# Leaving out the masked 64x64 blocks of a causal score matrix, with 64x64 transposes, in a fused retention and GELU kernel

## The chip, the cores and the metric

The kernel runs on one core of a Trainium2 chip. The time is device microseconds from one execution; three runs of the kernel before gave 203.04, 203.36 and 203.53 us, median 203.36. The profile is of a further execution. PE is TensorE (with PEld, its weight loads), DVE is VectorE, ACT is ScalarE, POOL is GpSimd and SP is SyncE, which issues most DMAs.

## The reference

Eight heads (H) of 64 channels (D), four sequences (B) of 768 tokens, in float32. First a recurrence with a decay for each head, then a feed-forward block on its output:

```python
for t in range(S):
    state = gamma[None, :, None, None] * state + einsum('bhd,bhe->bhde', k[:, :, t], v[:, :, t])
    y[:, :, t] = scale * einsum('bhd,bhde->bhe', q[:, :, t], state)
x = y.transpose(0, 2, 1, 3).reshape(B * S, H * D)
h = x @ w_in                                             # 512 x 2048
g = 0.5 * h * (1.0 + tanh(c * (h + 0.044715 * h**3)))
out = g @ w_out                                          # 2048 x 512
```

The recurrence is computed by chunks of tokens: inside a chunk, y is (q k^T, with decay and a causal mask) times v; what lies ahead of the chunk comes in through a state of 64x64 for each head.

## The kernel before

The tokens are cut into six chunks c of 128; a chunk of all four sequences (b = 0 to 3) is 512 rows of x. For each chunk there is an attention part and a MoE part, and the MoE matmuls of one chunk fill PE while the attention of the next waits for other engines.

**Attention of chunk c** (`att`, line 779). `load_in` (765) loads q, k and v of one b, 128 tokens x 8 heads x 64 floats, in one DMA each; in chunks 3 to 5 (`BLK`) `q_load` (704) loads q of all b in 16 DMAs (L713), in an order that lets DVE transpose it in 32x32 blocks (`trq`, L689). `cast` (226) makes f16 of it, with decay factors from the table `cst` by L234 or without by L217/L219. `mm_T` (266, L269) transposes q and k, two heads at a time, as 128x128 on PE; in chunks 3 to 5 only k. `evT`/`evTk` copy the transposes from PSUM into `qkT`. `mm_A` (273, L278) makes the scores: 16 matmuls for a b, each 64 channels x 64 keys x 128 queries, on one of the four 64x64 quarters of the array; the two heads of a pair (j) go to two PSUM banks. `ev_A1` (328, L329) multiplies them on DVE with `mask`, which holds the triangle and the decay, and writes `a` in f16. `mm_yc` (289, L297) starts y with state times q; `mm_yi` (306, L309) adds a times v, 8 matmuls of 128 keys x 64 channels x 128 queries for a b, two at a time on the two column halves. `ev_Y1` (331, L336) scales y with `dec` and writes `x`. `mm_s` (318, L320) makes k^T v for the new state, and `ev_S2` (338, L341) adds it.

**MoE of chunk c.** Chunk 0 and the first product of chunk 1 are plain matmuls (L407 and L553). The others are a seven-product scheme for 2x2 blocks (`PROD`, line 511): `m1w_mm` (525, L530) with its sums `xs` and `u_w`, GELU on ACT (L423), `m2w_mm` (539, L542) with sums `s_g` and `t_w` (L432, on DVE and POOL). Partial results go from PSUM by ACT copies (`snap`, L217, into `st` or `o`) and DVE adds (`add`, L432).

**What sets the order.** Every operation is an `Item` with needs, buffers and the engines that may do it (`KIND`, 600). The order and the engine of each are written out in the string `ORDER` (16): a letter for the engine, a number for the item. The code at line 1230 walks through it; a buffer or bank is taken from the slot that came free first. So each engine runs its instructions in a fixed order and waits at each for its inputs. SP issues its loads in one chain (`prev`). PSUM has eight bank slots; `SIZE` (129) holds the numbers of the other buffers, five of `qkT` among them.

Of the kernel before, what the change touches and what calls it, by code (L numbers as in the profile page):

```python
# [16 lines left out]
v8 g0 v9 p168 a167 a7 w3 p173 g10 g1 g2 p171 g3 g4 a172 p178 p184 w1 p188 a187 p176 v169  # L17
v170 p180 a179 p182 p190 a189 v174 p192 a191 v175 v181 p206 p208 v143 v147 v148 v151 v152
v159 v160 v139 a183 g5 p210 v135 v162 v154 p194 p186 p196 a177 a193 a185 a209 v144 p198 p212
a211 v163 p222 p224 a205 p200 p214 a197 a223 a199 p226 p202 g6 a213 s11 v23 v140 v141 s12  # L20
s13 p228 p230 s14 p232 a207 a201 v149 a229 a225 p216 a221 a227 s15 s16 g28 g25 a195 v24 s17
s18 s19 p204 a203 s20 s21 v164 a215 v26 v155 p803 p234 a233 p236 s22 g31 g34 p804 p805 s35
s36 p806 p807 v136 a235 s37 a231 p218 p808 p809 p220 p810 p811 a219 v27 s38 s39 s40 p238
v237 p812 a813 a217 p815 v146 a816 v156 p243 v242 p818 p241 v240 v239 p246 v245 p257 v244
p821 p822 p823 v29 v30 p260 v259 p262 a261 a819 v138 s41 s42 v32 v33 s43 v157 s44 s45 g57
g58 s46 s47 s814 p824 a825 v166 v150 v158 p248 p272 p274 a271 a273 p276 p253 a275 v247 v252
p278 a277 p280 a279 p256 v255 s820 p251 p258 v249 v250 p282 p284 a281 p268 v254 p264 a283
a263 a48 p266 a51 a52 v265 p270 v165 v269 a54 g55 v267 p286 p288 g49 p290 p325 a287 a289
g305 v303 v324 p335 p292 s60 s61 s62 g50 p320 s826 v304 v334 a285 v53 v56 a291 p330 a319
a329 p294 p296 p298 s63 a293 v307 v308 a295 p333 s64 s65 a297 g311 g312 g59 v332 p338 v336  # L30
p323 v337 p300 a299 p302 a301 v322 g313 v321 p827 p328 v331 p340 p339 v326 p342 g314 p348
p350 p352 v327 v341 v347 v351 p346 p344 g315 p828 a69 g71 v343 v137 v316 v345 g353 g355 s66
p830 p831 a829 a81 a73 s817 s67 a75 a77 g79 v142 p376 s68 p357 p374 a375 s85 p393 g354 p833
g318 v832 p834 g310 p391 s86 v349 p398 a392 g72 p381 g356 g80 s87 v145 v317 v394 a358 v377
a382 p379 a380 p396 p362 a363 a835 v78 p359 v360 v70 a361 a397 p836 p366 v153 g76 p386 p837
a83 a395 v309 p364 a365 p839 a378 v161 p400 p383 v387 g306 v367 v384 a399 a838 p369 p840
a368 a388 a385 v401 p403 p372 s88 s89 v370 a373 v404 p408 a409 p389 p406 g84 a405 p410 p415
a371 g425 g426 g427 a402 p452 a390 v82 a407 a416 v411 v74 g433 p842 p843 s90 p413 a414 a412
g434 p447 p442 a441 p457 v429 v841 a98 v844 s845 v446 p420 v451 v456 v421 g430 p417 p846
a422 a100 v418 p455 v453 p460 p445 v458 v443 v459 s91 p847 a848 v444 g97 p850 s92 v454 s849  # L40
p423 a424 a419 g428 g437 p851 a852 p450 p461 v448 p462 p472 p468 p464 p470 v449 v471 a94
g438 a106 p474 v463 v469 p466 v465 s93 p853 p854 p856 p857 g102 v467 g104 v435 p481 p530
p496 a497 s110 g475 p479 a480 p498 s111 a858 a96 g476 v439 g477 g436 v855 a108 v473 g101
g478 a531 v95 v499 s112 s113 s114 g119 g109 v482 p859 p503 p532 g432 g121 a504 a500 s115
s116 p501 a502 v533 p860 a534 p564 p484 v563 v99 v431 p508 v509 p486 p569 v568 v107 p535
a487 a485 p505 v506 a536 a861 p862 p488 a507 v489 p537 p863 v440 p491 v492 a483 a490 p539
a538 p579 a510 p494 p511 a512 g553 a495 p865 g105 a578 p513 p866 v540 v864 a514 v551 p515
v103 v120 p574 p520 a493 g547 a573 v516 a517 p518 a521 a519 g552 g122 g549 p542 p869 p686
a685 v867 v543 s117 s868 p525 v526 a527 p522 v523 s118 a544 a524 p870 a871 s872 p572 v571
a541 p582 g548 p528 a529 v580 p545 a546 g561 v581 v570 v555 v557 g556 v559 g560 g550 g562  # L50
g558 p873 p874 a875 p577 v575 a123 p567 v565 v576 v566 p876 p877 p584 p583 p594 p588 p592
p586 v124 v585 a131 a133 a127 a129 v587 p590 v589 g554 p596 v593 v591 p879 a125 p880 a881
v595 p882 p635 a636 v878 p601 a602 p603 p883 p618 a619 p691 v604 g597 p620 p625 g599 v132
v690 g598 p885 v621 g600 g134 p640 a605 p637 v638 a626 a884 p623 a624 p630 v631 p608 v128
p606 a622 p642 p627 v628 a609 a641 a639 a643 p652 p644 a607 v645 a646 a629 p886 v126 v887
p613 v614 a653 p647 p610 v611 a612 a615 v648 p888 p889 p654 v655 a632 p616 a617 g671 v130
p657 a658 p696 p633 p659 p701 v700 p661 p892 a634 v673 g674 g676 p650 v890 s891 a695 a660
v662 a656 a651 a649 g677 p694 v692 g678 g680 p689 v688 v687 p893 a894 v693 p664 v665 a666
p896 p667 a663 a668 p705 p708 p710 v707 v709 p699 v698 v697 g669 g681 p704 v703 v702 p897
a898 p721 p770 p899 a771 p736 g682 a737 p706 p712 p714 v713 v670 p900 v901 v711 g715 g717  # L60
p738 p753 v739 a740 a754 p902 p772 p903 a904 p743 a744 v773 p719 v679 p726 a720 v672 v722
v683 a727 v675 s895 p741 a742 v684 p758 a723 g716 p748 v749 p724 a725 p731 v732 a774 a733
a750 g718 p745 p905 p728 v729 v746 p906 p908 a730 a907 p775 p777 a778 p734 a735 p751 a776
g787 g788 a759 p909 g789 v910 p755 v756 p760 a761 p762 v763 p911 p912 p779 p782 p768 a752
a747 g791 v793 v913 s914 g792 g794 v783 a757 a769 p765 v766 a764 p915 a767 p916 g797 a784
v780 p785 a786 a781 a917 s918 v795 g801 v799 v796 g798 p919 p921 p923 a920 p925 a922 v800
p927 p929 a928 v790 a930 p931 p933 p935 v926 a932 a934 v802 p937 p940 v936 v938 s939 p943
p946 a947 p949 v924 v941 a942 a950 v944 s945 a948 s951
# [4 lines left out]
def kernel(  # L73
# [9 lines left out]
    nc = tc.nc  # L83
# [20 lines left out]
    gst_o = np.where(p_i[:, None] < 64, g128[None, 1::2], g128[None, 0::2])  # L104
    cst_np = np.concatenate([qdec, kdec, gst, gst_o, tri], axis=1).astype(np.float32)
# [16 lines left out]
    cst = const.tile([128, 192], F32)  # L122
    iden = const.tile([128, 128], F16)
# [10 lines left out]
        "qkT": (5, [128, 2, NHP, 128], F16),  # L134
# [9 lines left out]
    BLK = (3, 4, 5)  # L144
    ldq = const.tile([128, B, 4 * 128], F32, name="ldq")
# [80 lines left out]
    def cast(eng, nm, c, b):  # L226
        src = raw.pop((nm, c, b))
        sw = b if nm != "v" else 0
        o = h16[nm, c, b].rearrange("p (hp j) d -> p hp j d", j=2)
        if (nm == "v") == (c < 2):  # L230
            copy_on(eng, o, heads(src, sw))
        else:
            col = OQ if nm == "q" else OK
            eng.tensor_tensor(  # L234
                out=o,
                in0=heads(src, sw),
                in1=heads(cst[:, col:col + H].unsqueeze(2), sw).broadcast_to(
                    [128, NHP, 2, Dh]
                ),
                op=ALU.mult,  # L240
            )
# [30 lines left out]

    def mm_A(c, b, ps):
        t = qkT[c, b]
        for hp in range(NHP):
            for m in range(2):
                for j in range(2):
                    nc.tensor.matmul(  # L278
                        out=ps[j][m * 64:(m + 1) * 64, hp],
                        lhsT=t[j * 64:(j + 1) * 64, 1, hp, m * 64:(m + 1) * 64],  # L280
                        rhs=t[j * 64:(j + 1) * 64, 0, hp],
                        start=True,
                        stop=True,
                    )
# [42 lines left out]

    def ev_A1(eng, c, b, j, ps):
        eng.tensor_tensor(out=a_sb[c, b, j], in0=ps, in1=mask[:, j], op=ALU.mult)  # L329
# [24 lines left out]
    def o_evT(b, eng=nc.vector):  # L354
        qkT[0, b] = tile_of("qkT", b)
# [205 lines left out]
    def store(eng, o, p, c, a0, a1, n0=0, n1=512):  # L561
# [43 lines left out]
        add="v",  # L605
        evA="v",
        evY="v",
# [6 lines left out]
        evT="va",  # L614
        castq="ag",
# [12 lines left out]
        sume="gv",  # L628
        load="s",
# [43 lines left out]
    def q_cast(c, b):  # L673
# [13 lines left out]
        def tr(eng):  # L687
            qkT[c, b] = T["qkT", c, b]
# [5 lines left out]
        op("trq", tr, [("q16", c, b)], [("qT", c, b)], alloc=[(("qkT", c, b), 1)],  # L694
           early=[("al", "qkT", c, b)], free=[key])

    def load_dec():
        def emit(eng):
            eng.dma_start(out=dec.rearrange("p h t -> p (h t)"), in_=dec_h.ap())

# [19 lines left out]
    def cast_in(c, b, nm):  # L720
# [11 lines left out]
        last = c + 1 == NCk  # L732
        kind = "cast" if (nm == "v") == (c < 2) == (nm == "v") and (nm == "v" or c > 1) else "scale"
# [4 lines left out]
        if kind == "cast" and c in (1, 2) and False:  # L738
            kind = "castA"
        op(  # L740
            kind, emit,
# [23 lines left out]
    def load_in(c, b, nm):  # L765
        key = ("ld", nm, c, b)
        ldk = ld_key(c, b, nm)

        def emit(eng):
            eng.dma_start(  # L770
                out=T[ldk], in_=srcs[nm][b, :, c * C:(c + 1) * C, :].rearrange("h p d -> p h d")
            )

        shape = (SIZE["ld"][1],) if ldk[0] == "st" else ()
        op("load", emit, [prev[0]], [key], alloc=[(ldk, 1, *shape)],
# [14 lines left out]

# [482 lines left out]
```

## Time and profile before

| | |
|---|---|
| median of three runs | 203.36 us |
| the profiled execution | 201.71 us |
| its span, first to last instruction | 199.9 us |
| mean granted TensorE clock | 1.000 |
| PE busy, matmuls | 192.4 us, 2460 |
| PEld busy | 157.5 us |
| DVE, ACT, POOL busy | 151.7, 123.0, 108.7 us |
| transposes L269 (128x128) | 144, 128 of them in the `ps` banks |
| scores L278 (64x128 out, 64 rows) | 384 |
| a times v L309 (64x128 out, 128 rows) | 192 |
| state L320 / state times q L297 | 160 / 160 |
| score evacuations L329 on DVE | 48, 682 ns each |
| DMA | 30.11 MB, 170 GB/s of HBM traffic over the span |

PE's matmuls are pipelined: the time that one takes from PE is the distance to the start of the next, not its own duration. The matmul records give these distances; the timeline view joins neighbours of one line into one row.

### The profile page before, as it was taken

The numbers are of one execution on the slowest core, as the hardware profiler recorded it, in microseconds if no ns is written. First come the engines' busy times: TensorE is split into PE (matmuls) and PEld (weight loads), VectorE is DVE, ScalarE is ACT, GpSimd is POOL, SyncE is SP. The second block draws the span as 40 slices with busy tenths as digits, with TensorE's granted clock in tenths as the row PEclk, the third lists the DMA queues.
The fourth block names the chain that finished last, engine by engine and source line by source line (L and its number), as shares of the span: only waits on it lengthen the run. The fifth ranks groups of instructions, "written<-read, shape, count | busy, mean of one in ns | idle before, by whom it ended". The sixth has DMA issues, their size and how long they took to land.

```text
span 199.9 us, 5916 instructions
## 1 busy us (share of the span) xinstructions
PE 192.4 (96%) x2460; PEld 157.5 (79%) x2460; DVE 151.7 (76%) x278; ACT 123.0 (62%) x233; POOL 108.7 (54%) x109
## 2 busy tenths in 40 slices
PE   7999999989999999999999999999999999999993
PEld 2447895555889898789888899888988888888882
DVE  4366008599788999999999898899697879948730
ACT  2466474023578609999863889857779636786411
POOL 0657000021218575997899579898704967269500
PEclk9999999999999999999999999999999999999999
DMA  6999999998999779987996797610000500002204
GB/s 159 284 267 207 207 204 196 219 258 184 230 241 252 135 132 242 268 130 130 274 257 122 123 223 190 192 48 0 3 0 0 213 3 0 3 0 107 108 26 184
DMA packets 95898, 30.11 MB, mean 151 GB/s; under 512 B 88320, under 2 KB 92800, under 8 KB 95872
## 3 DMA queue, kind: packets, MB, share of 16 engines
q1 hardware_dynamic: 85120, 23.45, 50.6%
q0 software_dynamic: 4224, 4.19, 12.6%
q10 hardware_dynamic: 6528, 2.10, 4.2%
q8 instruction: 19, 0.31, 0.6%
q14 instruction: 7, 0.06, 0.1%
HBM read 27.64 MB, written 6.29 MB: 170 GB/s over the span
## 4 chain that ended last, share of the span: by engine, by line
PE 61%; DMA 14%; DVE 9%; SPq 7%; ACT 3%; POOL 2%; issue 1%; DVEq 0%; ACTq 0%
PE ps L542 26%; PE ps L530 20%; DMA w_out<-in_moe_w_out_dram 10%; PE ps L407 5%; SPq L713 4%; DMA ld<-in_v_dram 3%; SPq L164 3%; PE ps L269 2%; PE ps L278 2%; PE ps L309 2%; PE ps L553 2%; ACT qk L217 2%; DMA ldq<-in_q_dram 1%; DVE s_g L432 1%; DVE st L432 1%
## 5 line engine op out<-in xcount | busy, mean ns | idle before, releaser
L423 ACT ACTIVATE g<-ps 128x512 f16<-128x512 f32 (+1 forms) x56 | 28.3, 538 | 20.6 <-PE ps L407 16.8
L432 DVE TENSOR_TENSOR st<-ps,st 128x512 f32<-128x512 f32 x48 | 31.4, 680 | 5.9 <-PE ps L530 3.0
L542 PEld LDWEIGHTS <-s_g 128*128 128x128 f16 x320 | 31.1, 98 | 4.0 <-DVE s_g L432 0.4
L432 POOL TENSOR_TENSOR s_g<-g 128x512 f16<-128x512 f16 x21 | 24.7, 1184 | 16.9 <-ACT g L423 9.4
L423 ACT ACTIVATE g<-st 128x512 f16<-128x512 f32 x48 | 28.6, 629 | 8.2 <-DVE st L432 7.9
L217 ACT COPY st<-ps 128x512 f32<-128x512 f32 x48 | 26.5, 593 | 8.9 <-PE ps L530 8.8
L407 PE MATMUL ps<-x,w_in 128*128 128x256 f16 (+1 forms) x320 | 30.3, 251 | 0.1
L329 DVE TENSOR_TENSOR a<-ps,mask 128x512 f16<-128x512 f32 x44 | 27.3, 682 | 3.6 <-PE ps L278 3.5
L407 PEld LDWEIGHTS <-w_in 128*128 128x128 f16 x320 | 25.6, 98 | 3.4 <-DMA w_in<-in_moe_w_in_dram 0.3
L530 PEld LDWEIGHTS <-w_in 128*128 128x128 f16 x256 | 24.8, 98 | 3.3 <-issue 0.4
L542 PEld LDWEIGHTS <-g 128*128 128x128 f16 x240 | 22.9, 98 | 3.2
L217 ACT COPY o<-ps 128x512 f32<-128x512 f32 (+1 forms) x28 | 14.5, 528 | 13.8 <-PE ps L542 9.5
L530 PEld LDWEIGHTS <-u_w 128*128 128x128 f16 x192 | 18.5, 98 | 3.2 <-ACT st L217 0.7
L542 PE MATMUL ps<-w_out,s_g 128*128 128x256 f16 x160 | 19.9, 273 | 0.1
L542 PE MATMUL ps<-t_w,s_g 128*128 128x256 f16 x160 | 19.6, 273 | 0.0
L542 PE MATMUL ps<-w_out,g 128*128 128x256 f16 x160 | 19.5, 273 | 0.0
L530 PE MATMUL ps<-xs,u_w 128*128 128x256 f16 x128 | 17.8, 272 | 0.7 <-ACT st L217 0.4
L432 POOL TENSOR_TENSOR s_g<-s_g,g 128x512 f16<-128x512 f16 x14 | 16.3, 1169 | 3.8 <-DVE s_g L432 3.2
L530 PE MATMUL ps<-xs,w_in 128*128 128x256 f16 x128 | 18.4, 273 | 0.0
L432 POOL TENSOR_TENSOR s_g<-g,s_g 128x512 f16<-128x512 f16 x15 | 17.4, 1169 | 1.0 <-DVE s_g L432 0.8
L530 PE MATMUL ps<-x,w_in 128*128 128x256 f16 x128 | 17.4, 273 | 0.2 <-DVE st L432 0.2
L432 DVE TENSOR_TENSOR s_g<-g 128x512 f16<-128x512 f16 x19 | 15.2, 815 | 2.4 <-ACT g L423 2.1
(68 smaller groups left out, 289.7 us busy)
## 6 DMA issues: line engine op xcount, KB each, us to landing
ld<-in_v_dram SPq DMA_DIRECT2D x19, 256.0 KB, 4.3
ld<-in_k_dram SPq DMA_DIRECT2D x17, 256.0 KB, 4.4
out_dram<-o SPq DMA_DIRECT2D x8, 512.0 KB, 3.2
ldq<-in_q_dram SPq DMA_DIRECT2D x48, 64.0 KB, 2.7
w_in<-in_moe_w_in_dram POOLq DMA_DIRECT2D x4, 512.0 KB, 10.3
w_out<-in_moe_w_out_dram POOLq DMA_DIRECT2D x4, 512.0 KB, 15.1
ld<-in_q_dram SPq DMA_DIRECT2D x5, 256.0 KB, 4.5
out_dram<-o SPq DMA_DIRECT2D x5, 256.0 KB, 3.8
```

The costliest lines, as they stand in the source:

```text
L164: eng.dma_start(out=raw[nm, c, b], in_=srcs[nm][b, :, c * C:(c + 1) * C, :].rearrange("h p d -> p h d"),)
L217: eng.copy(out=out, in_=in_)
L269: nc.tensor.transpose(out=ps[:, i, hp], in_=pair(h16[nm, c, b], hp), identity=iden)
L278: nc.tensor.matmul(out=ps[j][m * 64:(m + 1) * 64, hp], lhsT=t[j * 64:(j + 1) * 64, 1, hp, m * 64:(m + 1) * 64], rhs=t[j * 64:(j + 1) * 64, ...
L309: nc.tensor.matmul(out=ps[j * 64:(j + 1) * 64, hp], lhsT=h16["v", c, b][:, 2 * hp + j], rhs=a_sb[c, b, j][:, hp], start=(c == 0), stop=Tru ...
L329: eng.tensor_tensor(out=a_sb[c, b, j], in0=ps, in1=mask[:, j], op=ALU.mult)
L407: nc.tensor.matmul(out=out, lhsT=w_in_sb[wi][:, kc, wr * 128:(wr + 1) * 128], rhs=xT[c][:, kc, t0:t1], start=(kc == 0), stop=(kc == NHP - ...
L423: nc.scalar.activation(out=out, in_=in_, func=AF.Gelu_apprx_tanh, scale=1.0)
L432: eng.tensor_tensor(out=out, in0=in0, in1=in1, op=op)
L530: nc.tensor.matmul(out=ps[:, f], lhsT=m1_lhs(lk, kc, 2 * g + f), rhs=x[:, kc], start=(n in FIRST and kc == 0 and f == 0), stop=(n in (1, 5 ...
L542: nc.tensor.matmul(out=ps, lhsT=m2_lhs(c, lk, fp, a), rhs=m2_rhs(rk, fp), start=(first and fp == 0), stop=(n in (1, 5, 6) and fp == NP - 1 ...
L713: eng.dma_start(out=t[p0:p0 + 32, :, a, :], in_=src[j, dd, t0:t0 + 32])
```

## The change

For chunks 2 to 5 (`SW = 2`) the scores of early queries against late keys, a 64x64 block of each head that the mask makes zero, are no longer computed. For heads 0 to 3 keys 0 to 63 of the chunk stay on partitions 0 to 63; for heads 4 to 7 the token halves of k and v are swapped, so that the early keys, which meet all 128 queries, lie on partitions 64 to 127. k is swapped by its cast, now three operations; v by its load, now three DMAs. The score tile shrinks from 128x512 to 128x384 and so does its evacuation, with a new mask made of a new table `cs2`. From chunk 1 on transposes are 64x64, four at a time, into two banks; a-times-v uses 64x64 quarters with half the keys each, in two turns over a pair of b, and between the turns a one-element copy (`peek`) reads the last column of the first turn. `qkT` has two buffers of two b each instead of five of one. `ORDER` is new throughout. The core of the diff:

```diff
-        "qkT": (5, [128, 2, NHP, 128], F16),
+        "qkT": (2, [128, 2, 2, NHP, 128], F16),
...
+    SW = 2
...
+        if nm == "k" and c >= SW:
+            i = heads(src, sw)
+            copy_on(eng, o[:, 0:2], i[:, 0:2])
+            copy_on(eng, o[0:64, 2:4], i[64:128, 2:4])
+            copy_on(eng, o[64:128, 2:4], i[0:64, 2:4])
+        elif (nm == "v") == (c < 2):
             copy_on(eng, o, heads(src, sw))
         else:
-            col = OQ if nm == "q" else OK
+            tab = cst[:, OQ:OQ + H] if nm == "q" else (cs2 if c >= SW else cst[:, OK:])[:, 0:H]
...
+    def mm_T2(c, bs, ps, nms):
+        for n, b in enumerate(bs):
+            for i, nm in enumerate(nms):
+                for hp in range(NHP):
+                    for m in range(2):
+                        rows = slice(m * 64, (m + 1) * 64)
+                        for j in range(2):
+                            nc.tensor.transpose(
+                                out=ps[m][j * 64:(j + 1) * 64, n + i, hp],
+                                in_=h16[nm, c, b][rows, 2 * hp + j],
+                                identity=iden[rows, rows],
+                            )
+
+    def halves(c, hp):
+        if c < SW:
+            return (0, 0, slice(0, 128), hp), (1, 64, slice(64, 128), hp)
+        far = hp > 1
+        return (far, 0, slice(0, 128), hp % 2), (1 - far, 64, slice(128, 192), hp % 2)
+
+    HPS = (0, 2, 1, 3)
+
     def mm_A(c, b, ps):
         t = qkT[c, b]
-        for hp in range(NHP):
-            for m in range(2):
+        for hp in HPS:
+            for m, t0, cols, x in halves(c, hp):
+                if c < SW:
+                    t0, cols = 0, slice(0, 128)
                 for j in range(2):
                     nc.tensor.matmul(
-                        out=ps[j][m * 64:(m + 1) * 64, hp],
+                        out=ps[j][m * 64:(m + 1) * 64, x, cols],
                         lhsT=t[j * 64:(j + 1) * 64, 1, hp, m * 64:(m + 1) * 64],
-                        rhs=t[j * 64:(j + 1) * 64, 0, hp],
+                        rhs=t[j * 64:(j + 1) * 64, 0, hp, t0:],
...
+    def mm_yi2(c, bs, ps, turn):
+        for hp in HPS if turn == 0 else HPS[::-1]:
+            for m, t0, cols, x in halves(c, hp):
+                for j in (0, 1) if turn == 0 else (1, 0):
+                    b = bs[m ^ j ^ turn]
+                    nc.tensor.matmul(
+                        out=ps[b][j * 64:(j + 1) * 64, hp, t0:],
+                        lhsT=h16["v", c, b][m * 64:(m + 1) * 64, 2 * hp + j],
+                        rhs=a_sb[c, b, j][m * 64:(m + 1) * 64, x, cols],
+                        start=False,
+                        stop=(turn == 1),
+                        skip_group_check=True,
+                    )
...
     def ev_A1(eng, c, b, j, ps):
-        eng.tensor_tensor(out=a_sb[c, b, j], in0=ps, in1=mask[:, j], op=ALU.mult)
+        m = mask2 if c >= SW else mask
+        eng.tensor_tensor(out=a_sb[c, b, j], in0=ps, in1=m[:, j], op=ALU.mult)
...
+            for rows, hs, at in (
+                (slice(0, 128), slice(0, 4), t0),
+                (lo, slice(4, 8), t0 + 64),
+                (hi, slice(4, 8), t0),
+            ):
+                n = rows.stop - rows.start
+                eng.dma_start(
+                    out=T[ldk][rows, hs],
+                    in_=srcs[nm][b, hs, at:at + n, :].rearrange("h p d -> p h d"),
+                )
...
+            def peek(eng):
+                b = bs[halves(c, HPS[-1])[1][0] ^ 1]
+                copy_on(eng, misc[64:65, 1:2], T["bank", "Y", c, b][64:65, HPS[-1], C - 1:C])
```

In the table of engines the peek may go to DVE or ACT, the k cast to ACT or POOL, the two operations that make the new mask to DVE or POOL.

## The prediction

> **What bounds the kernel now.** I read the engine totals first, then the waits of TensorE (PE), then PE's timeline around the attention steps, then the two queues that feed it. Engine totals and the chain's shares (the page):
>
> ```profile
> PE 192.4 (96%) x2460; PEld 157.5 (79%) x2460; DVE 151.7 (76%) x278; ACT 123.0 (62%) x233; POOL 108.7 (54%) x109
> ...
> PE 61%; DMA 14%; DVE 9%; SPq 7%; ACT 3%; POOL 2%; issue 1%; DVEq 0%; ACTq 0%
> ```
>
> PE is busy 96% of the span; the chain's other shares lie mostly before 45 us and between 62 and 86. The waits of PE (total, times, longest):
>
> ```profile
> PE ps L278 <- DVE qkT L219: 0.6, 1, 0.6
> ...
> PE ps L530 <- ACT st L217: 0.4, 1, 0.4
> PE ps L530 <- POOL xs L432: 0.2, 1, 0.2
> PE ps L530 <- DVE st L432: 0.2, 1, 0.2
> PE ps L320 <- DVE a L329: 0.2, 1, 0.2
> ```
>
> After the start-up PE waits for almost nothing. Start to start in the matmul records, the gaps beyond streaming and beyond the mode changes below add up to 3.2 us after 20 us. So the time follows the sum of PE's stream, and the change is priced there first. The granted clock is 1.000 throughout. PE's timeline (start, us, instructions; a row's length holds the tail of its last matmul):
>
> ```profile
> 125.76 0.82 PE L542 MATMUL ps<-t_w,g 128*128 128x256 f16 x6
> 126.51 0.64 PE L278 MATMUL ps<-qkT 64*64 64x128 f16 x32
> 127.08 1.05 PE L530 MATMUL ps<-xs,w_in 128*128 128x256 f16 x8
> ```
> ```profile
> 49.25 0.61 PE L269 MATMUL ps<-iden,qk 128*128 128x128 f16 x8
> 49.69 2.78 PE L407 MATMUL ps<-x,w_in 128*128 128x256 f16 x24
> ```
> ```profile
> 133.27 0.44 PE L320 MATMUL ps<-v,qk 128*64 128x64 f16 x16 [0.19 <-DVE a L329]
> 133.52 1.09 PE L309 MATMUL ps<-a,v 128*64 128x128 f16 x32
> 134.42 0.44 PE L320 MATMUL ps<-v,qk 128*64 128x64 f16 x16
> ```
>
> The reader is to see four prices. (1) A 128x128 transpose: 8 in 0.44 us (49.25 to 49.69), **56 ns** each, with no gap to its 128*128 neighbours. (2) L278's 64*64 matmuls run four at a time, one on each quarter of the array: inside the group starts are 3 to 4 ns apart, and a group of four with 128 columns takes **56 ns**. (3) L320's N=64 matmuls run two at a time, **31.5 ns** a pair, and L309's N=128 pairs take 56. (4) A **change of array shape** costs: 32 matmuls of L278 are 8 groups, 448 ns, but hold PE for 574; the gap in front is 203 ns where L542's own is 109, and the first gap behind is 119 for 109. That is 230 ns for an excursion, 115 a change; over the whole trace 51 changes cost 5.9 us.
>
> **The change, part by part, on PE.** The counts are those of the built programs' PE order.
> - Transposes of chunks 1 to 5: 112 of 128x128 go (112 x 56 = 6.27 us); 448 of 64x64 come, 112 groups of four with N=64. No row shows four N=64 matmuls at once. Below, a group can't beat half of L278's 56, 28 ns; above, it takes no more than L278's 56, which has the same number of weight loads and starts. I take 31.5, L320's N=64 pair, the nearest row in N: 3.53 us, so -2.74 (from -3.14 to 0).
> - Scores (L278) of chunks 2 to 5: in each of 64 groups one half of the columns now has N=64. The head order 0, 2, 1, 3 puts the short half on alternating sides, so two heads take 56 + 31.5 instead of 112: 32 x 24.5 ns = -0.78.
> - a times v (L309): 160 matmuls, 80 pairs at 56 ns, become 320 in 80 groups. Chunk 1 is not swapped, and its 16 groups stay at 56 by the m=0 half; in chunks 2 to 5 the 64 groups alternate as above: -0.78. These two bounds are 0 and -0.9 each, by the same N=64 price.
> - Array changes: T2, scores, yc and a-times-v share the 64*64 shape now, but T2 leaves the 128*128 shape of the MoE matmuls. Counted along the order: 51 become 76. (One more warm-up matmul at the start stands where PE waited anyway.) 25 x 115 ns = **+2.88**.
>
> Sum on PE: -4.31 + 2.88 = **-1.4 us**. As a formula: 176 short halves save 56 - q each, q being the time of an N=64 group; the 25 changes eat the gain at q = 40.
>
> Here a rule of the Trainium skill speaks against the change. L320's loads in the same half follow each other after 31.5 ns, and the second four loads of L278's run come 28 ns behind the first. The Trainium skill ("TensorE: Matmul & The Clock Gate", section LDWEIGHTS) gives a load as its columns divided by 1.2, in ns, whatever the rows: 64 columns would be an estimated 53 ns, a group of N=64 would not get below it, and the PE sum would be an estimated +2.4 instead of -1.4. The rows of this trace disagree by nearly half.
>
> **Waits that come or go.**
> - The peek: turn 1 of a-times-v adds to the PSUM columns of turn 0 from the other row half, so a one-element copy on DVE (6) or ACT (4) reads turn 0's last column and PE waits for it: ten times. Round trip by rows: L278's last matmul at 8.69 us to its DVE reader 0.26; the copy at most 0.22 (DVE 128x128, L204; ACT 128x1 0.20); DVE end to PE 0.05. About 0.5 us. In the order there lies between the turns: L320's 32 matmuls with two changes (0.73 us) in four, 8 of L542 (1.1 us) in three, 16 (2 us) in two, 64 transposes (0.5 us) in one. So it is covered if the copy's engine is free; one evacuation of 0.5 us ahead of it costs up to 0.3 in the five short ones. Without cover ten cost 5. Behind a waiting peek on DVE stand the x evacuations, which free the Y banks and feed POOL's xs; behind the waiting matmul stands all of PE. Taken: +0.5 (0 to 1.6).
> - The 0.83 us at 44.5 (L278 behind DVE's qkT copy, the longest wait of PE after 20 us): each T2 of chunk 1 is followed by 8 of the 128x512 matmuls (1.73 us) before its scores, and two ACT copies (0.58 each) fit in. -0.8. Late next on DVE would be the casts of b = 2 and 3, which by L234's spacing of 0.6 end at 48.0, as PE arrives.
> - SP: v's loads go from 1 to 3 DMAs, 32 more issues at L713's spacing of 0.53 us, 17 us. SP issues almost without pause from 37 to 120 us. Chunk 2's four v loads took 56.4 to 61.5, about the DMA engines' pace (share 1.02 there); 12 issues take 6.4, cs2 0.5 more. So q of chunk 3 lands some 1.8 us later, and ACT waits for it in its queue, with the st copies behind:
>
> ```profile
> 75.24 0.62 ACT L217 CAST qk<-ldq 128x512 f16<-128x512 f32 x1 [5.57 <-DMA ldq<-in_q_dram]
> 75.77 0.58 ACT L217 COPY o<-ps 128x512 f32<-128x512 f32 x1
> 76.37 2.50 ACT L217 CAST qk<-ldq 64x512 f16<-64x512 f32 x4
> ...
> 79.94 2.52 ACT L217 COPY st<-ps 128x512 f32<-128x512 f32 x5
> ```
>
>   In the new order only five ACT operations, not eight, stand between that landing and the first st copy: 77.0 + 5 x 0.55 = 79.8 for 79.94. Taken +0.4 (0 to 2), for the three-part k casts that ACT now has among the st copies. Later loads have over 10 us: chunk 5's v is issued by 126, and L309 first uses it at 158.
> - DVE: 32 score evacuations of 128x384: by the 128x512 (682 ns) and 128x256 (420) rows 551 each, -4.2 us. Six peeks (at most 1.3), the two halves of the new mask (0.68 + 0.42), two more s_g sums (1.6), a net of half a us of copies and casts: the total stays near 151, and so nothing is gained from DVE. k's casts: 16 go from one operation to three; on ACT 0.62 becomes about 1.17 (3 x 0.39, the 256-column row), seven times, +3.9 on an engine at 62%; POOL's nine lie beside work at 54%. If that cover is gone, it shows as a late k transpose.
>
> Sum: -1.4 - 0.8 + 0.5 + 0.4 = **-1.3 us**. The profiled execution took 201.71 us (span 199.9 and 1.8 around it), 1.65 below the median 203.36. So span 198.6, profiled 200.4, median **202.1**.
>
> **Rivals.**
> - *Short groups do not shrink* (slower): q stays near 56, because weight loads and starts, not columns, set it. For it: no row keeps up eight instructions in under 56 ns. Against: L320's pairs. (The Trainium skill's rule on loads, above, would lead here too.) Then PE +2.9, and with the waits +0.1: 206.4. With the waits it is slower from q = 39 on; at 45, 204.4.
> - *Peek and ACT waits are exposed*: PE and the old wait give -2.2, uncovered peeks 5 and late st copies 2: 208.2 at worst, 204.7 with half of it; slower from 2.2 us of new waits on. For it: DVE is 91 to 97% busy in the stretches from 60 to 110 us. Against: the covers above.
> - *More waits go*: q = 28 and the other 2.4 us of old gaps vanish too: 203.36 - 2.05 - 3.2 = 198.1 at best, 199.7 with half of the gaps. For it: DVE's evacuations shorten just ahead of PE. Against: DVE's total stays.
> - *It does not do what it says*, scores and a-times-v save no columns because the starts wait in order for the long half; the transposes keep their gain: 203.36 + 2.88 - 2.74 + 0.1 = 203.6. Against: at 134.42 us an N=64 matmul of L320 starts 27 ns behind a long one in the other half.
>
> **How the numbers follow.** Forecast 0.57 (its own range 201 to 203.1), short groups 0.14, exposed waits 0.14, more waits gone 0.09, columns not saved 0.06. About 0.2% (0.4 us) is what a measurement here can tell from no change. Faster: most of the forecast (0.50) and the third rival, with a little of the second: 0.61. Same: 0.05 of the forecast, half of the fourth rival, some of the second: 0.11. Slower: 0.28. The range 200.5 to 205.2 leaves out half of the third rival and the upper ends of the first two.
>
> **What would show it.** T2 groups at 31.5 ns (8 groups in about 0.25 us), 76 array changes at 115 ns, score runs of 32 in 0.35 us of streaming, PE waits on misc under 1 us in total, DVE's score row at 0.55 us, the wait at 44 us gone. T2 groups over 40 ns, or PE idle behind misc or st of over 3 us, would make the forecast wrong.

## The result, and the profile after

The kernel after takes **219.82 us** (median of six runs, 215.97 to 221.82); the kernel before took 203.68 on the same chip (six runs, 203.04 to 205.53). The ratio is **1.066**, 95% interval 1.054 to 1.079: slower, where 1.3 us less was forecast, and outside the range of 200.5 to 205.2. The ratios here and below leave out executions that are over 1.5% above the fastest of their kernel; for the kernel after that leaves two of the six (215.97 and 219.02), so that the loss is 13.5 us by the ratio and 16.1 by the medians. The profiled execution took 220.77 us, the second longest of the six, its span 218.8, against 201.71 and 199.9 before.

The page of the kernel after: engine totals, and the granted clock in 40 slices.

```profile
PE 194.8 (89%) x2957; PEld 155.2 (71%) x2957; DVE 146.4 (67%) x292; ACT 126.3 (58%) x252; POOL 116.3 (53%) x128
...
PEclk9999599999999999958999999999999999999999
```

PE was busy 96% of the span and is now busy 89%, and the clock, full throughout before, drops at two places. The waits of PE (total, times, longest) name both:

```profile
PE ps L603 <- DVE st L505: 5.7, 1, 5.7
PE ps L362 <- POOL v L232: 5.4, 1, 5.4
```

In the matmul records PE's own spacing, array changes included and waits left out (gaps that exceed the usual spacing by some 60 ns or more), is 187.7 us before and 186.9 after. So the stream did shrink, by 0.8 us; with a closer limit for what is a wait it is up to 1.2. The waits, with the matmuls at half clock behind them, grew from 7.4 to 25.8 us, and 3.9 of these are the half clock. That is +18.4 and -0.8, and with 1.2 us more behind PE's last matmul it makes up the 18.9 us by which the span grew, but for rounding. The reader should see that the change failed outside the engine it was made for.

**The wait at 94 us.** PE's row, and ACT's in front of it:

```profile
94.37 2.74 PE L603 MATMUL ps<-xs,u_w 128*128 128x256 f16 x12 [5.68 <-DVE st L505]
```
```profile
89.49 2.53 ACT L230 CAST qk<-ldq 128x512 f16<-128x512 f32 x4 [9.84 <-DMA ldq<-in_q_dram]
```

ACT stands still for 9.8 us at the cast of q of chunk 3; the st copies are in its queue behind that cast, DVE's adds need the copies, and PE needs the banks. Before, the same cast waited 5.6 us and PE hardly noticed. Why q came late is in SP's own rows (start, us held, DMAs):

```profile
65.38 8.76 SPq L866 DMA_DIRECT2D ld<-in_v_dram  x12
74.23 1.02 SPq L636 DMA_DIRECT2D out_dram<-o  x2
75.36 10.97 SPq L794 DMA_DIRECT2D ldq<-in_q_dram  x16
```

Before, the four v loads took SP 5.0 us from 56.4 on and the 16 q loads 8.9, done at 72.7; now they are done at 86.3. Of these 13.6 us, 8.9 were there when the v loads began: the chain of loads started at 37.8 instead of 25.8, because the kernel holds it back for a GELU result of chunk 0, which came late through the wait at 24.65 us. PE itself was late by that wait too; e1 below shows what remains without it.

**The wait at 24.65 us.** PE waits 5.4 us for the f16 cast of v of chunk 0, b = 3, on POOL; POOL waits for the load. SP issued that load at 8.87 (7.87 before), and it landed at 23.94 (14.65 before). Nothing in the change touches this load. The stretch from 5 to 10 us (busy time of the engines, granted clock, DMA share, GB/s), before and after:

```profile
5.00:10.00 5.00, 4.54 (x44) 2.25 (x43) 1.74 (x3) 2.01 (x3) 3.03 (x4) 1.00 1.26 285
```
```profile
5.00:10.00 5.00, 3.01 (x35) 1.42 (x33) 1.06 (x2) 1.53 (x2) 1.77 (x2) 1.00 1.38 218
```

The same loads run at 218 instead of 285 GB/s while the DMA engines are busier. In the packet records a 256-byte packet takes 18 ns (median) there before and 25 after, 34 at the 90th percentile. What differs is the place in memory: `cs2` has 208 floats, 832 bytes on each partition, so every tile allocated behind it moved to 64 bytes past a multiple of 256 (`ldq` from byte 19712 to 20544); before, all lay on multiples of 256. The Trainium skill ("DMA: Bandwidth & Descriptors", section "How a descriptor splits into AXI transactions") says that a transaction has to start on a 256-byte boundary, and that a descriptor which starts elsewhere also pays for the bytes between; it says so of reading, while here the side that is written has moved. The packet times go the same way, though not for all packets: in most later stretches the median stays at 18 ns and only the 90th percentile rises.

Slower packets alone do not make v nine microseconds late. In the packet records POOL's first weight load (`w_in`, packets of 1024 bytes on a queue of its own) begins to move at 15.2 us, and at 13.2 before. At that moment 309 KB of the start-up loads are still to come, where it was 116 KB before. From 17 to 21 us they move at about 40 GB/s beside 155 GB/s of weights, some 150 packets of each kind in a microsecond. At the 218 GB/s of the stretch from 5 to 10 us the 309 KB would have taken 1.4 us, by an estimate; they took 8.4. So the loads were slowed just enough to meet the weights, and the meeting cost the most.

**Theories.** S: SP's issue time for v's three-part loads makes q and the output stores late. P: the new table's size moved the tiles, and the loads of the start-up became slower. O, a rival to both: the new order is itself worse. T, another: the transposes, array changes or peeks cost more than priced.

### The profile page after: what moved, and what is told of

It is laid out like the page before. It is cut to its first block, busy times and chain, and to the rows that moved or that the text cites. A ratio compares the mean times of both kernels' runs of the same rounds, so it can differ in the third digit from the quotient of the medians.

```text
span 218.8 us, 7019 instructions
## 1 busy us (share of the span) xinstructions
PE 194.8 (89%) x2957; PEld 155.2 (71%) x2957; DVE 146.4 (67%) x292; ACT 126.3 (58%) x252; POOL 116.3 (53%) x128
## 4 chain that ended last, share of the span: by engine, by line
PE 62%; DMA 13%; DVE 8%; SPq 8%; ACT 3%; issue 2%; POOL 1%; ACTq 0%; POOLq 0%
PE ps L615 20%; PE ps L603 20%; PE ps L480 10%; DMA ld<-in_v_dram 8%; PE ps L626 7%; SPq L794 4%; SPq L177 2%; DVE s_g L505 2%; SPq L866 2%; DMA ldq<-in_q_dram 2%; DMA st<-in_q_dram 2%; ACT qk L230 2%; PE ps L320 2%; DMA out_dram<-o 1%; PE ps L375 1%
## 5 line engine op out<-in xcount | busy, mean ns | idle before, releaser
L505 DVE TENSOR_TENSOR st<-ps,st 128x512 f32<-128x512 f32 x48 | 31.8, 682 | 13.2 <-PE ps L603 8.7
L505 POOL TENSOR_TENSOR s_g<-g 128x512 f16<-128x512 f16 x23 | 27.1, 1186 | 16.8 <-ACT g L496 16.6
L496 ACT ACTIVATE g<-st 128x512 f16<-128x512 f32 x48 | 29.1, 642 | 7.4 <-DVE st L505 7.3
L400 DVE TENSOR_TENSOR a<-ps,mask 128x384 f16<-128x384 f32 (+1 forms) x44 | 23.5, 585 | 5.5 <-PE ps L320 5.4
L603 PEld LDWEIGHTS <-u_w 128*128 128x128 f16 x192 | 19.1, 102 | 9.1 <-DVE st L505 6.0
L603 PE MATMUL ps<-xs,u_w 128*128 128x256 f16 x128 | 19.0, 287 | 5.7 <-DVE st L505 5.7
L615 PE MATMUL ps<-w_out,s_g 128*128 128x256 f16 x160 | 21.1, 281 | 0.0
L505 POOL TENSOR_TENSOR s_g<-s_g,g 128x512 f16<-128x512 f16 x15 | 17.3, 1158 | 1.9 <-DVE s_g L505 1.5
L230 ACT CAST qk<-ldq 64x512 f16<-64x512 f32 (+3 forms) x18 | 10.4, 581 | 12.0 <-DMA ldq<-in_q_dram 9.8
L252 POOL TENSOR_TENSOR v<-ld,cs 128x512 f16<-128x512 f32 x13 | 13.7, 1057 | 4.7 <-DMA ld<-in_v_dram 4.5
## 6 DMA issues: line engine op xcount, KB each, us to landing
w_out<-in_moe_w_out_dram POOLq DMA_DIRECT2D x4, 512.0 KB, 11.4
```

What stands on the lines that cost most here:

```text
L230: eng.copy(out=out, in_=in_)
L252: eng.tensor_tensor(out=o, in0=heads(src, sw), in1=heads(tab.unsqueeze(2), sw).broadcast_to([128, NHP, 2, Dh]), op=ALU.mult,)
L400: eng.tensor_tensor(out=a_sb[c, b, j], in0=ps, in1=m[:, j], op=ALU.mult)
L496: nc.scalar.activation(out=out, in_=in_, func=AF.Gelu_apprx_tanh, scale=1.0)
L505: eng.tensor_tensor(out=out, in0=in0, in1=in1, op=op)
L603: nc.tensor.matmul(out=ps[:, f], lhsT=m1_lhs(lk, kc, 2 * g + f), rhs=x[:, kc], start=(n in FIRST and kc == 0 and f == 0), stop=(n in (1, 5 ...
```

## The experiments

Each batch ran beside the kernel before on the same chip: 202.61 us for e1 to e4, 202.88 for e5 to e8, 202.64 for e9 to e12. Intervals are of the ratio to it.

**e1: after, with `cs2` padded to 1024 bytes.**

```diff
-    cs2 = const.tile([128, 16 + 192], F32)
+    cs2w = const.tile([128, 256], F32)
+    cs2 = cs2w[:, 0:208]
```

> The changed kernel with one edit: the tile of the new table cs2 is 1024 bytes a partition instead of 832 (the last 192 bytes unused), so that every later tile starts on a multiple of 256 bytes again, as in the kernel before. Theory A (placement): in the profile of the changed kernel 256-byte DMA packets take 25 to 34 ns in the first 15 us, for 18 throughout in the kernel before, because the 832 bytes put all load targets 64 bytes past such a multiple; the last v of chunk 0 then lands at 24 us instead of 14.7, PE stands still for 5.4 us, the clock is halved for 6.8 us, the load chain starts 12 us later, and ACT and then PE wait for q of chunk 3. It expects packets at 18 ns, no wait of PE over 1 us before 30 us, and 202 to 206 us in all. Rival B (order and loads): the new table and the 32 extra v loads make the two long waits; it expects 214 us or more and both waits still there.

213.12 us (210.73 to 214.71), ratio 1.050 (1.039 to 1.062). Packets are back at 18 ns, the rate at 5 to 10 us at 288 GB/s, the wait for v is gone, and the chain of loads starts at 29.0. The waits on q (6.5 us at 86.5) and behind a peek (2.2 at 141.8) stay. So one of the two long waits was P's. Theory A's 202 to 206 us was missed, since the other wait stays, and rival B, which has both stay, fails by the first. How much of the loss is P's is known only roughly: 6.7 us by the medians, 3.3 by the ratios (1.066 and 1.050, whose intervals overlap). The runs of the two kernels don't overlap, but they are from different chips.

**e2: before, with an unused tile of 64 bytes.**

```diff
     cst = const.tile([128, 192], F32)
+    shift = const.tile([128, 16], F32)
```

> The kernel before with one edit: an unused tile of 64 bytes a partition behind the table cst, so that every later tile starts 64 bytes past a multiple of 256. Theory A expects packets of 25 ns or more in the first 15 us, the last v of chunk 0 late by several us, and 210 to 218 us. Rival B expects no change: 203 to 205 us, packets at 18 ns.

210.13 us, ratio 1.030 (1.018 to 1.043). The tile is never written or read, and it costs 6.1 us by the ratio, 7.5 by the medians. Its packets take 25 ns (34 at the 90th percentile) at 5 to 10 us, and PE waits for the same v:

```profile
PE ps L321 <- POOL v L220: 2.8, 1, 2.8
```

When the weights begin to move, at 15.5 us, 194 KB of the start-up loads are still to come, and v lands at 20.6. P is shown, in a kernel without anything else of the change.

**e3: e1 with 128x128 transposes, into one bank, copied out in the same two parts.**

```diff
-                    for m in range(2):
-                        rows = slice(m * 64, (m + 1) * 64)
-                        for j in range(2):
-                            nc.tensor.transpose(
-                                out=ps[m][j * 64:(j + 1) * 64, n + i, hp],
-                                in_=h16[nm, c, b][rows, 2 * hp + j],
-                                identity=iden[rows, rows],
-                            )
+                    nc.tensor.transpose(
+                        out=ps[:, n + i, hp], in_=pair(h16[nm, c, b], hp), identity=iden
+                    )
```

> As e1_pad, with the transposes of chunks 1 to 5 again as 128x128 (112 at 56 ns) into one bank, and nothing else changed: the swapped and shortened scores stay. The array changes fall from 76 to 68. The prices of the prediction say against e1_pad: transposes +2.7 us, eight changes less at 0.115 us -0.9, so +1.8 on PE (theory P, the price of a short group is right). Rival: 64x64 transposes bring nothing in the whole, within 0.4 us of e1_pad or faster than it, because PE's stream is no longer what sets the end.

211.46 us, ratio 1.041 (1.029 to 1.053); e1's interval overlaps it, so the time doesn't tell. The stream does: 188.3 us without waits, 1.2 more than e1. (The built order has 64 array changes, not the 68 of the expectation; with 64 the prices give +1.4.) So the 64x64 transposes are worth what was priced. Its profiled execution, 216.2 us, is the longest of its five and holds a 6.0 us wait for v at 22.9 us, with packets at 18 ns up to 12 us. There the weights begin to move early, at 12.3 us, with 320 KB of the start-up loads still to come; v's packets beside them take 31 ns, and it lands at 22.2. So that load can meet the weights on a boundary too; being off it slows the loads and so brings the meeting about, but is not its only cause.

**e4: e1 with v of chunks 2 to 5 in one DMA each** (the token halves of v are not swapped).

```diff
-            if not swap:
+            if True:
```

> As e1_pad, but v of chunks 2 to 5 comes in one DMA of 256 KB for each b again. The token halves of heads 4 to 7 of v are then not swapped, which leaves that part of the change out. Four v loads of chunk 2 held SP for 5.1 us in the kernel before and for 8.8 in the changed one. Theory S (SP's issue time delays q of chunk 3 and so ACT and PE) expects 2 us or more less than e1_pad. Rival: with the tiles on multiples of 256 bytes the loads are in time either way, within 0.5 us of e1_pad.

204.59 us, ratio 1.010 (1.005 to 1.015). 32 DMAs fewer on SP give 8.5 us on the same chip. Both waits of e1 are gone; the ones of over 1 us that remain after the start-up are new and of another kind, and the first two stand behind qkT copies on DVE:

```profile
68.42 0.44 PE L299 MATMUL ps<-iden,qk 64*64 64x64 f16 x30 [1.14 <-DVE qkT L233]
...
98.93 0.54 PE L321 MATMUL ps<-qkT 64*64 64x64 f16 x30 [1.30 <-DVE qkT L233]
```

**e5: before, in its old order, with v of chunks 2 to 5 in three DMAs.**

```diff
+                for lo, hi, hs in ((0, 128, slice(0, 4)), (0, 64, slice(4, 8)), (64, 128, slice(4, 8))):
+                    eng.dma_start(
+                        out=T[ldk][lo:hi, hs],
+                        in_=srcs[nm][b, hs, c * C + lo:c * C + hi, :].rearrange("h p d -> p h d"),
+                    )
```

> The kernel before, its order of work untouched, with v of chunks 2 to 5 loaded by three DMAs each (heads 0 to 3 of all rows, then heads 4 to 7 of each half of the rows, same tokens, nothing swapped): 32 more DMAs on SP and nothing else. Theory S (SP's issue time is the price of the split): 32 issues at the 0.53 us that SP's q loads show are 17 us on a queue that has no pause from 26 to 120 us; q of chunk 3 then lands 4 to 7 us later and PE waits for it behind ACT, +4 to +9 us, 207 to 212. Rival O (the three-part load hurts only in the new order, which has fewer ACT operations between the q cast and the st copies, and swaps k in the casts): within 1.5 us of before.

209.63 us, ratio 1.036 (1.030 to 1.041): the split alone costs 6.75 us in the old order, as theory S has it. The rival, that it hurts only in the new one, falls. SP issues the 12 v loads in 9.2 us instead of 5.0. That this is issuing and not the moving of the data is seen in the DMA engines: during the 9.2 us they are busy 0.70 of the time (168 GB/s), during the 5.0 us before 0.94 (225 GB/s). ACT's and PE's rows show the two ways in which lateness on SP arrives, q behind a load and an output tile behind a store:

```profile
78.15 0.62 ACT L217 CAST qk<-ldq 128x512 f16<-128x512 f32 x1 [8.23 <-DMA ldq<-in_q_dram]
```
```profile
110.47 0.58 ACT L217 COPY o<-ps 128x512 f32<-128x512 f32 x1 [5.29 <-DMA out_dram<-o]
```
```profile
79.31 1.91 PE L542 MATMUL ps<-t_w,s_g 128*128 128x256 f16 x16 [2.36 <-ACT o L217]
...
111.11 0.81 PE L542 MATMUL ps<-t_w,s_g 128*128 128x256 f16 x6 [2.89 <-ACT o L217]
```

**e6: e1 with only chunk 2's v in one DMA each** (not swapped there).

```diff
-        swap = c >= SW and nm == "v"
+        swap = c > SW and nm == "v"
```

> The aligned kernel after (e1) with only the v of chunk 2 in one DMA each, chunks 3 to 5 in three (leaves out the swap of token halves of chunk 2). Theory S with its first place at 86 us: the 6.7 us wait of PE behind the q of chunk 3 goes, since the 8 issues ahead of these q loads go (about 4 us), and the shorter waits of PE on the peek at 141 us stay: 205.5 to 208.5. Rival: the backlog on SP is a sum over all chunks, and the wait comes back at the q of chunk 4: 210 to 213.

208.46 us, ratio 1.029 (1.024 to 1.035): the wait at 86 us goes, as expected, and with it about 4 us. But the backlog comes back further on. SP, ACT and PE:

```profile
125.76 7.12 SPq L867 DMA_DIRECT2D ld<-in_v_dram  x9
132.98 1.06 SPq L637 DMA_DIRECT2D out_dram<-o  x2
```
```profile
138.00 0.59 ACT L231 COPY o<-ps 128x512 f32<-128x512 f32 x1 [8.34 <-DMA out_dram<-o]
138.61 0.15 ACT L231 COPY misc<-ps 1x1 f32<-1x1 f32 x1
```
```profile
138.81 0.53 PE L376 MATMUL ps<-a,v 64*64 64x128 f16 x16 [5.01 <-ACT misc L231]
```

The store of an output tile stands on SP behind nine v loads of chunk 5; ACT's copy into that tile waits for the store; the peek waits behind the copy; PE waits for the peek. The wait did not come back at q of chunk 4, as the rival had it, but the rival's point, that the backlog is a sum over all chunks, holds.

**e7: e1 with v in one DMA and its halves swapped in the scaling.**

```diff
+            for o0, o1, i0, i1, h0, h1 in (
+                (0, 128, 0, 128, 0, 4), (0, 64, 64, 128, 4, 8), (64, 128, 0, 64, 4, 8)
+            ):
+                eng.tensor_tensor(
+                    out=h16[nm, c, b][o0:o1, h0:h1],
+                    in0=src[i0:i1, h0:h1],
+                    in1=cst[i0:i1, OK + h0:OK + h1].unsqueeze(2).broadcast_to([i1 - i0, 4, Dh]),
+                    op=ALU.mult,
+                )
```

> The aligned kernel after with v in one DMA again and the token halves of heads 4 to 7 swapped in v's scaling instead, which goes from one operation (POOL 1.08, DVE 0.69 us) to three (128x256, 64x256, 64x256). Nothing of the computation is left out. Theory S: SP's 32 issues go, so the 8.5 us between e1 and e4 come back but for what POOL's longer scalings cost: by POOL's casts, one of 0.61 became 0.45 and two of 0.41, so about +0.7 us on each of 13, beside work at 57%: 204.5 to 207. Rival: POOL and DVE are as tight as SP, and v late costs what q late did: 209 to 213.

208.94 us, ratio 1.030 (1.024 to 1.035), above what S expected and all but in the rival's range. SP is relieved, but the scaling on POOL grows from 1.08 to 1.90 us for each v (0.65 and twice 0.62), 10.6 us in all, and PE waits 2.1, 1.4 and 1.3 us behind DVE and 1.2 behind POOL. The swap was paid in both places where it was put.

**e8: e4 with k cast by one operation** (k and v both unswapped).

```diff
-            i = heads(src, sw)
-            copy_on(eng, o[:, 0:2], i[:, 0:2])
-            copy_on(eng, o[0:64, 2:4], i[64:128, 2:4])
-            copy_on(eng, o[64:128, 2:4], i[0:64, 2:4])
+            copy_on(eng, o, heads(src, sw))
```

> e4 (aligned, v of chunks 2 to 5 in one DMA) with k of chunks 2 to 5 cast by one operation each, too (leaves out the swap of token halves for heads 4 to 7 in both k and v). It asks where the 2 us by which e4 stands above the kernel before come from. Theory K (the three-part k casts delay the transposes and the copies behind them on ACT): 202.5 to 203.5, the 1.5 us waits at 68 and 99 us gone. Rival D (they come from where the new order places the qkT copies behind the s_g sums on DVE): 204 to 205, the waits unchanged.

204.82 us, ratio 1.009 (1.004 to 1.015), the same as e4. The waits at 68 and 99 us went, as theory K has it, but one of 2.6 us behind DVE's st adds came at 82.5. So the three-part k casts cost no time that shows in the end, and neither theory gave the waits right.

**e9: e1 with four output stores issued by ACT.** Four letters of the order, s859, s863, s882, s886, become a.

> The aligned kernel after (e1, 213.1) with the four output stores of chunks 1 and 2 issued by ACT at the same places of the order instead of by SP. In e1 PE waits 2.4 us at 141.8 behind a peek on ACT, and in e6 5.2 us at 138.8: the peek stands in ACT's queue behind a copy to the output tile, which waits for the store of that tile, and that store stands on SP behind v's loads. Theory Q (the store is late only because SP's queue is): the 2.4 us go, and the four issues that leave SP take 2 us from the q of chunk 4 but none from the wait at 86 us, since only one pair of stores stands ahead of it: 209.5 to 211.5. Rival: ACT, holding the stores' waits in its own queue, loses as much: 212.5 or more.

227.56 us, ratio 1.125 (1.120 to 1.130): far worse than either theory. SP's and PE's waits:

```profile
SPq L795 <- DMA out_dram<-o: 16.1, 2, 10.0
```
```profile
PE ps L616 <- POOL s_g L506: 14.9, 3, 9.4
```

SP's q loads now wait for stores that ACT issued. No data joins the two, but a semaphore does: the instruction records show that the program gives the DMAs of SP and ACT eight semaphores in turn, and that a DMA waits until the one that had its semaphore before has landed. The q load at 105.13 us takes semaphore 109 from ACT's store, which landed at 105.11; the one at 134.99 takes 102 from the store that landed at 134.97. So the run says nothing about Q; it shows that moving a DMA to another queue can tie the two queues together.

**e10: e1 with the four peeks of ACT on DVE.** a480, a602, a724, a727 become v.

> The aligned kernel after (e1, 213.1) with all ten peeks on DVE (the four on ACT moved, at the same places of the order). Theory P (a peek costs only what stands ahead of it in its engine's queue): the 2.4 us wait at 141.8 goes, as DVE's queue holds nothing that waits for a store; 210 to 212. Rival: the copy to the output tile that waits on ACT blocks the st copies behind it too, and PE waits for these instead, a few us later: 212.5 to 214. If round trips themselves cost, the peeks on DVE show waits of over 0.5 us each.

213.75 us (211.83 to 217.11), ratio 1.056 (1.046 to 1.066): not to be told from e1. PE's waits on peeks fall from 2.2 to 1.2 us over three, the longest 0.8. But ACT's copy to the output tile still waits 4.1 us for the store, and PE waits 1.2 us at 148.9 where e1 had no such wait. The peek only passed on a lateness that was there, as the rival says.

**e11: e1 with no chunk in the swapped layout.**

```diff
-    SW = 2
+    SW = 6
```

(and the new mask is not made).

> The aligned kernel after with the boundary of the swapped layout moved from chunk 2 to chunk 6, so no chunk uses it: v in one DMA, k cast by one operation, scores of full width and evacuated at 128x512, the masked block still left out of a times v but with its short groups on one side, and the 64x64 transposes, the peeks and the new order kept. Nothing of the computation is left out. It is e8 with the columns put back: PE +1.6 by the prices (0.8 for scores, 0.8 for a times v), DVE +4.3 (32 evacuations at 0.68 instead of 0.55). Theory: 206 to 208, PE's stream 1.5 longer than e8's 186.5 and some of DVE's 4.3 us seen as waits. Rival (short columns save nothing, as starts set the pace): 204.5 to 205.5 with the same stream.

206.01 us, ratio 1.019 (1.014 to 1.025), 1.4 us above e4. PE's stream is 188.3 us, 1.8 more than e8's 186.5, where 1.6 was priced. The short columns save what was worked out. DVE's 4.3 us more are hardly seen: the waits are 10.3 us, for e8's 11.4, of which 1.6 are matmuls at half clock behind its wait at 82.5.

**e12: e4 with the qkT copies before 68 and 99 us ahead of DVE's sums.** In the order, `a328 v339 p306 a305 v334 v333` goes ahead of `v317 v312`, and `v161 v443 g444` behind `v456`.

> e4 (aligned, v in one DMA, without the swap of v's token halves: 204.6) with a few places of the written order moved: the qkT copies on DVE before 68 and 99 us go ahead of the s_g and w_in sums that stand before them there (1.3 us each while POOL works). Theory D (the 2 us by which e4 stays above the kernel before are the order's qkT copies placed late on DVE): the waits of 1.8 and 1.5 us go, 201.5 to 203. Rival: the sums, now later, make PE wait for s_g instead, or the waits come back at the next copy: 204 to 205.5.

203.36 us, ratio 1.003 (0.998 to 1.008). The waits at 68 and 99 us are gone (1.8 and 1.5 us counted from start to start), 1.2 us of the time with them; a wait of 1.0 us behind DVE came at 81.6. Without the swap of v, on a boundary and with two places of the order mended, the new kernel can't be told from the old one: in the profiled executions its PE stream is 1.2 us shorter and its waits are 2.7 us longer.

No run of the changed kernel, with all of its computation or without a part, beats the kernel before.

## Why the prediction was wrong, by its own steps

**PE's stream: right.** Consecutive rows of the kernel after:

```profile
75.76 0.45 PE L298 MATMUL ps<-iden,qk 64*64 64x64 f16 x32
76.03 0.52 PE L320 MATMUL ps<-qkT 64*64 64x128 f16 x32
76.49 1.92 PE L615 MATMUL ps<-w_out,g 128*128 128x256 f16 x16
```

Eight groups of transposes take 0.275 us from the first start to the next row's: the first step takes 53 ns, the seven others 31.7 each, where 31.5 was taken. The 32 score matmuls take 0.46, less one array change of 0.11: 0.35, as forecast. There are 76 changes at 0.111 us. The sum came to -0.8 in the kernel after and -0.9 in e4, for -1.4. Of what is missing, 0.2 is the one more warm-up matmul, which the stream counts; the first step of 53 ns behind a change is another part, and the rest was not followed up. The rule of the Trainium skill that was weighed there ("TensorE: Matmul & The Clock Gate", section LDWEIGHTS; an estimated 53 ns for 64 columns) would have given an estimated +2.4. The runs refute it as a bound on short groups, which follow each other after 31.7 ns with their loads.

**SP's queue: the step that failed.** "12 issues take 6.4, cs2 0.5 more. So q of chunk 3 lands some 1.8 us later". SP's rows before, and in e1, where the tiles are on a boundary:

```profile
56.44 5.04 SPq L770 DMA_DIRECT2D ld<-in_v_dram  x4
63.89 8.85 SPq L713 DMA_DIRECT2D ldq<-in_q_dram  x16
```
```profile
56.96 8.59 SPq L867 DMA_DIRECT2D ld<-in_v_dram  x12
66.78 12.26 SPq L795 DMA_DIRECT2D ldq<-in_q_dram  x16
```

Even there the 12 issues took 8.6 us (0.72 each, not 0.53), the 16 q loads behind them 12.3 instead of 8.9, and q's issue ended at 79.0 instead of 72.7: 6.3 us late, not 1.8. (Without the split, in e4, it ended at 75.3.) The price of one issue was read from q's loads and did not hold for v's partial ones. For q's own it held but for three of the 16 in e1: these held SP for 1.5 to 1.8 us instead of 0.49, each together with a 16 KB packet of the queue that the page of the profile calls `instruction` (at 66.75, 71.17 and 75.86 us), where the kernel before had one longer issue, of 0.9. So of the 6.3 us, 3.6 come from v's partial loads and 3.4 from these pauses, less 0.7 for what stands ahead and between. Why SP pauses at such packets no run shows; the prediction had no term for it. And "Later loads have over 10 us" looked at loads alone: the output stores are in the same queue, and from 133 us on they were late (e6). The prediction counted the 17 us that 32 issues take on a queue "almost without pause" and then charged 0.4 for them. What they cost in time is 8.5 us by e4 and 6.75 by e5. The cover that it counted, five ACT operations instead of eight, was used up by the 1.8 us that it allowed.

**`cs2`: costed as one issue, 0.5 us.** Its size was the cost: 3 to 7 us (e1), 6 to 7.5 in the old kernel (e2), from where the tiles behind it lie. No term of the sum asked where a new tile puts the others.

**The wait at 44.5 us (-0.8): not gained.** In e4 shorter gaps take its place: 0.34, 0.29 and 0.14 us from start to start at the transposes and a-times-v between 41 and 49 us, and 0.2 us ahead of the scores at 43.96.

**Peeks (+0.5): right where ACT is free.** The waits of PE in e4 list none. The 1.3 us in the kernel after and the 5.0 in e6 are a late store, passed through ACT.

**DVE: better than said, and worth nothing.** Score evacuations take 547 ns (551 priced), and the total fell to 146.4 where "near 151" was said. e11 puts the wide evacuations back and shows hardly more waits. DVE's load didn't matter; the places of single copies did (e12).

**k's casts: hidden,** as taken (e8).

**Rivals.** "Peek and ACT waits are exposed" named the right path, st copies late behind ACT's q cast, but with 2 us for them where the kernel after showed 5.7, and no rival had memory placement in it. Short groups that do not shrink and columns not saved are refuted by the stream. "More waits go" was not seen: the waits grew.

In sum, by the ratios and in steps from the kernel after to the one before: 3.3 us from placement (after to e1), 8.2 from the split (e1 to e4) and 1.9 that are left, which the order makes and in which PE's gain of about 1 us is already counted. These steps add up to the 13.5 us by their nature; that each part would cost as much in another sequence was not measured.

## What to carry to other kernels

When a change adds DMAs to a queue, price the queue as an engine: its busy stretch, how far each load and each store in it is ahead of its use, and a cost per issue taken from like issues. When it adds a tile, look at the byte at which the tiles behind it start; padding the odd one took 192 unused bytes a partition here. And a matmul saving on a full PE counts only after every queue that feeds it has been asked for slack.

## What was not expected of the hardware

- 64 unused bytes cost 3% (e2, 1.8 to 4.3%): 256-byte packets at 64 bytes past a 256-byte boundary took 25 to 34 ns instead of 18 in the busiest stretches.
- Loads of 256-byte packets lose most of their rate beside loads of 1024-byte packets on another queue: the start-up loads fell from 218 GB/s (287 in e3) to about 40 beside the weights' 155.
- A wait of PE costs more than itself. The granted clock fell to 0.50 within the 5.4 us wait, from 21.2 to 28.05 us, and within the 5.7 us one, from 92.9 to 99.7, and behind them 256-column matmuls followed each other after 213 ns instead of 109. That was 3.9 us in all. Waits of 2.1 to 2.6 us in e1, e7 and e8 brought 3.4 us at 0.50 each.
- On POOL a 64x256 piece of v's scaling takes 0.62 us and a 128x256 piece 0.65 (e7): half the partitions save nothing.
- SP's long issues fall on 16 KB packets of the `instruction` queue: a q load took 0.49 us to issue as a rule, and of the 49 that took over 1.1 us in all fourteen profiles 43 overlap such a packet.
